# Sliding-window attention with a GeGLU branch: P times V by 64-key halves in two PSUM banks, row maxima in quarters of the TensorE array

## Chip, cores and metric

One core of a Trainium2 chip runs the whole kernel. The metric is the device time of one execution in microseconds (us), lower is better. The kernel before has a median of 1067.9 us over three runs (1067.76 to 1069.48).

Engines are named as the profile names them: PE is TensorE (PEld its weight loads), DVE VectorE, ACT ScalarE, POOL GpSimd, SP the engine that issues most DMAs. PE multiplies a moving operand by stationary weights, adds into PSUM banks, and can be split into row tiles (by the contracted dimension) and column tiles (by the output's partitions).

## What is computed

```python
def _A_ref(x, wqkv, wo):
    B, S, D = x.shape                       # 1, 2048, 640
    H = 32; Dh = D // H; W = 256            # 32 heads of 20, window of 256 keys
    qkv = (x @ wqkv).reshape(B, S, 3, H, Dh).transpose(2, 0, 3, 1, 4)
    q, k, v = qkv[0], qkv[1], qkv[2]
    scores = einsum("bhqd,bhkd->bhqk", q, k) * (Dh ** -0.5)
    mask = (0 <= idx[:, None] - idx[None, :]) & (idx[:, None] - idx[None, :] < W)
    p = softmax(where(mask, scores, -1e9), axis=-1)
    o = einsum("bhqk,bhkd->bhqd", p, v)
    return o.transpose(0, 2, 1, 3).reshape(B, S, D) @ wo

def _B_ref(x, w_gate, w_up, w_down):        # Df = 1728
    return (gelu(x @ w_gate) * (x @ w_up)) @ w_down

xn = layernorm(x)
return x + _A_ref(xn, ...) + _B_ref(xn, ...)
```

A query sees itself and the 255 keys before it, so only a band of the scores is computed.

## The kernel before

**Stages.** The first 60 us or so normalise and transpose x and start the projections. Then the attention stage (some 100 to 645 us in the profile) runs attention and the projections together. After it come the rest of the gate and up products and the output products. The change lies in the attention stage and in one mask that is built at the start.

**Units and slots.** Attention is cut into 32 units: 8 groups of 4 heads, times 4 chunks of 512 queries. `attention()` writes the order of PE, ACT, DVE and POOL out by hand: what the Python emits first stands first in each engine's queue. A unit has 14 slots (`NS`). In every slot come first the deferred actions that fall due (`tick`, filled by `defer(n, ...)`, n slots later), then the maxima, P times V and exp work of that slot, then about three steps of filler (`pull_fill(RATE / NS)`): matmuls of the projections and of the gate and up products, which are long, full-array f32r matmuls (L105).

**Maxima.** `max_pair(u, i)` (L458) computes the scores of two heads for 128 queries, only to find each query's maximum. The two heads lie in two row halves of the array (60 rows each, `tile_position=(64 * r, 0)`) and write two PSUM banks of `psm`, which has four. The band of 128 queries is 384 keys wide; where it reaches into the previous chunk the keys come from that chunk's tile in a matmul of their own. DVE adds the mask and reduces in one custom instruction for each head (L477). `pull_max(2, T)` emits two such calls at slots 0, 0, 4 and 8: the second of slot 0 behind P times V. So two calls take all four banks. The stream of maxima runs some units ahead.

**Exp.** `exp_piece(u, s)` (L518) computes the scores of one head again, transposed (keys on partitions), into a bank of `psx`, which has two, and ACT writes exp into a P tile (f32, 128 keys x 4 heads x 512 columns). A unit has three P tiles X, Z and Y of several key blocks each (`pieces`), so 12 pieces, two in every even slot from 0 to 10. One slot after a tile's last piece `clear` sets what lies outside the band to zero, on POOL (L545, L548). In slot 0 one step of filler stands between the two pieces.

**P times V.** `av_unit(u - 1)` (L551) runs in slot 0 between the two pulls of maxima. For each key block (128 keys on the partitions), for each of the 4 heads, one f32 matmul adds v-transposed times P into the head's 32 partitions of one `psx` bank `o` (column tiles 0, 32, 64, 96; the 21st row of v is ones and gives the sum). A chunk above 0 has six key blocks, with 384, 128, 256, 256, 384 and 128 queries; chunk 0 has four, with 384, 256, 384 and 128. ACT copies `o` to `ob`, and three slots later SP stores it with five DMAs.

Of the kernel before, what the change touches and what calls it, by code (L numbers as in the profile page):

```python
# [19 lines left out]
C = 512  # L20
# [7 lines left out]
NEG = -3.0e38  # L28
SR = 3 * DH
# [36 lines left out]
def block_kernel(ctx, tc, x, wqk, wv, wgu, wdo, wdl, out):  # L66
    nc = tc.nc
# [41 lines left out]
    def dense(*a):  # L109
        for _ in dense_steps(*a):  # L110
# [8 lines left out]
    qkp = pa.enter_context(tc.tile_pool(name="qkp", bufs=2))  # L119
    pr = ExitStack()  # L120
    vp = pr.enter_context(tc.tile_pool(name="vp", bufs=5, side="right"))
    st1 = pr.enter_context(tc.tile_pool(name="st1", bufs=1, side="right"))
    identb = st1.tile([128, 256], BF, name="identb")[:, 0:128]
    nc.gpsimd.tensor_copy(identb, ident)
    mask = st1.tile([128, 384], F32, name="mask")
    nc.gpsimd.memset(mask, 0.0)
    nc.gpsimd.affine_select(out=mask, in_=mask, pattern=[[1, 384]], compare_op=OP.is_ge,
                            fill=NEG, base=-1, channel_multiplier=-1)
    nc.gpsimd.affine_select(out=mask, in_=mask, pattern=[[-1, 384]], compare_op=OP.is_ge,
                            fill=NEG, base=256, channel_multiplier=1)  # L130
# [327 lines left out]
    def max_pair(u, i):  # L458
        g, c = divmod(u, NC)
        jj, b = divmod(i, 4)  # L460
        q, k = qs[u % NQ], ks[u % NK]
        if i == 0:
            maxes[u] = ap.tile([128, 4, 4], F32, name="mx", tag="mx")
        pss = [psm.tile([128, 384], F32, name="ps_m", tag="mx") for _ in range(2)]
        old = max(0, 256 - 128 * b) if c else 0
        n0 = max(0, 128 * b - 256)
        n = old + 128 * b + 128 - n0
        parts = [(0, old, ks[(u - 1) % NK], C - old, C)] if old else []
        parts.append((old, n, k, n0, 128 * b + 128))
        for lo, hi, kt, k0, k1 in sorted(parts, key=lambda p: p[1] - p[0]):  # L470
            for r, ps in enumerate(pss):
                rows, j = slice(64 * r, 64 * r + SR), 2 * r + jj
                nc.tensor.matmul(ps[:, lo:hi], q[rows, j, 128 * b:128 * b + 128], kt[rows, j, k0:k1],  # L473
                                 start=True, stop=True, tile_position=(64 * r, 0))
        junk = ap.tile([128, 384], BF, name="junk", tag="junk", bufs=1)
        for r, ps in enumerate(pss):
            nc.vector.tensor_tensor_reduce(out=junk[:, 0:n], in0=ps[:, 0:n], in1=mask[:, 384 - n:384], scale=1.0,  # L477
                                           scalar=NEG, op0=OP.add, op1=OP.max,
                                           accum_out=maxes[u][:, 2 * r + jj, b:b + 1])
# [70 lines left out]

    def av_unit(u):  # L551
        g, c = divmod(u, NC)
        o, v = psx.tile([128, C], F32, name="ps_o", tag="ex"), vtiles[g]
        todo = [(pts[u, bi], *p) for bi, bank in enumerate(pieces(c)) for p in bank]
        for i, (pt, kb, col, q0, n) in enumerate(todo):
            assert (id(v), kb) in done, (u, kb)
            for j in range(4):
                w0_ = kb * 84 + 21 * j
                nc.tensor.matmul(o[32 * j:32 * j + 32, q0:q0 + n], v[:, w0_:w0_ + 32], pt[:, j, col:col + n],  # L559
                                 start=i == 0, stop=i == len(todo) - 1, skip_group_check=True,  # L560
                                 tile_position=(0, 32 * j))
        ob = ap.tile([128, C], F32, name="ob", tag="ob", bufs=1)
        nc.scalar.activation(ob, o, AF.Copy)  # L563

        def store():
            for j in range(4):
                nc.sync.dma_start(od[c].rearrange("(d h) t -> h d t", h=H)[4 * g + j], ob[32 * j:32 * j + DH, :])
            nc.sync.dma_start(sd[c][4 * g:4 * g + 4, :], ob[DH::32, :])

        defer(3, store)  # L570

    def load_gu(f):
        raws = []
# [181 lines left out]
    def attention():  # L755
        now[0] = -1
        load_stack(0)
        load_stack(1)
        load_stack(2)
        for i, (p, k, half) in enumerate((p, k, half) for p in range(NC // 2) for k in range(2) for half in range(2)):  # L760
            for j, fn in enumerate(x_sums(p, k, half)):
                at(XS0 + XSN * i + 2 * j, fn)
        for i in range(12):
            now[0] = i - 13
            for fn, a in tick():
                fn(*a)
            if i % 2 == 0:
                pull_max(2, now[0])
            flush()
            pull_fill(2 * RAMP)  # L770
        pull_fill(GAP)
        for u in range(NU + 1):
            for i in range(NS):
                T = now[0] = NS * u + i
                for fn, a in tick():
                    fn(*a)
                if i in (0, 4, 8) or T == 2:
                    pull_max(2, T)
                if i == 0 and u:
                    av_unit(u - 1)  # L780
                    flush()
                    pull_max(2, T)
                if i % 2 == 0 and i < 12 and u < NU:
                    exp_piece(u, i)
                    if i == 0 and u:
                        pull_fill(1)
                        debt[0] -= 1
                    exp_piece(u, i + 1)
                flush()
                if u + 3 < NU and i in (KSLOT, 12):  # L790
# [661 lines left out]
```

## Time and profile before

| | |
|---|---|
| median of three runs | 1067.9 us |
| span of the profiled execution | 1070.0 us |
| instructions in the profile | 21147 |
| mean granted TensorE clock | 0.995 |
| P times V (L559): instructions, PE time | 1408, 84.3 us |
| maxima (L473): instructions, PE time | 704, 67.0 us |
| reductions on DVE (L477) | 512, 272.6 us |
| eviction of P times V on ACT (L563) | 32, 19.1 us |

The profile is one execution. A group's busy time counts overlapping instructions once, so the mean duration of one times the number is more than the busy time where several run at once. Matmuls are pipelined: the duration of one includes its way through the array, and what it costs in a row of others is read from differences of shapes or from the chain. The chain of waits follows the work that ended last back to what released it; its pieces are times that the end depended on.

### The profile page before, as it was taken

Reading aid. Unit: us, or ns where it says so; the run is one execution under the profiler, and the core shown is the slowest. Engines: PE = TensorE matmul, PEld = TensorE weight load, DVE = VectorE, ACT = ScalarE, POOL = GpSimd, SP = SyncE. Lnnn points to the kernel's source line nnn. Section 1 sums busy time; section 2 is a strip of 40 time slices with the busy share of each in tenths; the row PEclk is TensorE's granted clock in tenths of the full one; section 3 lists DMA queues with packets and bytes.
Section 4 is the critical chain, followed back from the end, with each engine's and each line's share of the span. In section 5 each row is a group of like instructions: output and inputs, shape, how many; then the busy total and the mean of one; then the engine's idle time right before and its main releaser. Section 6 shows DMA issues by size and latency. Waiting matters only on the chain.

```text
span 1070.0 us, 21147 instructions
## 1 busy us (share of the span) xinstructions
PE 1055.2 (99%) x7253; PEld 830.4 (78%) x7253; DVE 746.0 (70%) x1985; ACT 518.8 (48%) x1088; POOL 337.8 (32%) x514
## 2 busy tenths in 40 slices
PE   8999999999999999999999999999999999999998
PEld 8877666666677766666666668888888999999998
DVE  7845667665565566776767716787776879888887
ACT  4434565566556565565556565332234544433332
POOL 5021564767554383736346340211100000000000
PEclk9999999999999999999999999999999999999999
DMA  5642344446452244424334116576677873443443
GB/s 196 189 131 85 114 135 126 145 131 187 131 153 86 86 120 139 150 85 134 96 116 130 55 60 198 172 245 207 244 247 240 274 261 120 129 131 109 132 132 104
DMA packets 105172, 158.46 MB, mean 148 GB/s; under 512 B 15420, under 2 KB 60092, under 8 KB 105064
## 3 DMA queue, kind: packets, MB, share of 16 engines
q1 hardware_dynamic: 102680, 150.95, 44.5%
q10 hardware_dynamic: 2384, 6.16, 1.8%
q8 instruction: 57, 0.93, 0.4%
q14 instruction: 51, 0.42, 0.1%
HBM read 101.78 MB, written 54.92 MB: 146 GB/s over the span
## 4 chain that ended last, share of the span: by engine, by line
PE 86%; DVE 7%; DMA 2%; ACT 2%; issue 2%; POOL 1%; SPq 0%; ACTq 0%; DVEq 0%; POOLq 0%
PE ps_d L105 27%; PE ps L1168 16%; PE ps_g L901 15%; PE ps_e L532 8%; PE ps_o L559 6%; PE ps_v L105 6%; PE ps_m L473 5%; DVE junk L477 2%; PE ps_g L105 1%; DMA hr<-hd 1%; DVE ss L1006 1%; PE ps_t L180 1%; DVE wt L1006 1%; DVE at L1006 1%; ACT wb L987 1%
## 5 line engine op out<-in xcount | busy, mean ns | idle before, releaser
L477 DVE CUSTOM_DVE_ANT_0 junk<-ps_m,mask 128x384 bf16<-128x384 f32 (+2 forms) x512 | 272.6, 532 | 150.5 <-PE ps_m L473 92.7
L534 ACT ACTIVATE P<-ps_e 128x512 f32<-128x512 f32 (+2 forms) x384 | 198.5, 569 | 93.6 <-PE ps_e L532 79.9
L1168 PE MATMUL ps<-wb,at 128*128 128x320 f32 x999 | 156.7, 309 | 1.1 <-DVE xr L1191 0.7
L1168 PEld LDWEIGHTS ps<-wb,at 128*128 128x128 f32 x999 | 148.9, 188 | 2.1 <-issue 0.9
L545 POOL TENSOR_SCALAR_AFFINE_SELECT P<-P 128x512 f32<-128x512 f32 x128 | 86.1, 672 | 168.0 <-ACT P L534 165.7
L105 PE MATMUL ps_d<-xh,wql 128*128 128x512 f32 x430 | 130.5, 415 | 0.0
L105 PE MATMUL ps_d<-xh,wqh 128*128 128x512 f32 x430 | 129.2, 413 | 0.0
L105 PE MATMUL ps_d<-xl,wqh 128*128 128x512 f32 x430 | 129.2, 412 | 0.0
L532 PE MATMUL ps_e<-qs,ks 124*128 124x128 bf16 (+2 forms) x704 | 117.7, 279 | 0.2 <-ACT ob L563 0.2
L532 PEld LDWEIGHTS <-ks 124*128 124x128 bf16 x704 | 49.6, 98 | 60.5 <-issue 51.1
L105 PEld LDWEIGHTS ps_d<-xl,wqh 128*128 128x128 f32 x430 | 80.1, 191 | 14.8 <-issue 0.8
L105 PEld LDWEIGHTS ps_d<-xh,wql 128*128 128x128 f32 x430 | 80.0, 191 | 13.8
L105 PEld LDWEIGHTS ps_d<-xh,wqh 128*128 128x128 f32 x430 | 79.1, 189 | 15.0 <-ACT xh L188 1.4
L1168 PE MATMUL ps<-wt,at 128*128 128x320 f32 x552 | 89.2, 310 | 0.8 <-DVE xr L1191 0.8
L559 PE MATMUL ps_o<-P,v 128*32 128x384 f32 (+2 forms) x1408 | 84.3, 386 | 0.0
L1168 PEld LDWEIGHTS ps<-wt,at 128*128 128x128 f32 x552 | 82.9, 188 | 1.3 <-DVE xr L1191 1.0
L548 POOL TENSOR_SCALAR_AFFINE_SELECT P<-P 128x512 f32<-128x512 f32 x112 | 72.9, 661 | 28.7 <-ACT P L534 28.7
L1122 ACT ACTIVATE at<-ss 128x512 fp32r<-128x512 f32 x59 | 37.3, 632 | 88.3 <-DVE ss L1006 88.3
L244 POOL TENSOR_TENSOR pt<-r,pt 128x512 bf16<-128x512 f32 x40 | 46.6, 1164 | 90.7 <-ACT pt L243 76.9
L559 PEld LDWEIGHTS ps_o<-P,v 128*32 128x32 f32 x1408 | 41.4, 110 | 39.7 <-issue 25.1
L473 PE MATMUL ps_m<-ks,qs 60*128 60x128 bf16 (+1 forms) x704 | 67.0, 275 | 4.8 <-DVE mx L477 3.1
L563 ACT ACTIVATE ob<-ps_o 128x512 f32<-128x512 f32 x32 | 19.1, 597 | 93.2 <-PE ps_o L559 80.1
(189 smaller groups left out, 1682.4 us busy)
## 6 DMA issues: line engine op xcount, KB each, us to landing
hr<-hd SPq DMA_DIRECT2D x104, 128.0 KB
hd<-he SPq DMA_DIRECT2D x50, 256.0 KB
wr<-wgu SPq DMA_DIRECT2D x27, 320.0 KB
qs<-qd SPq DMA_DIRECT2D x64, 120.0 KB
ks<-kd SPq DMA_DIRECT2D x64, 120.0 KB
xi<-x SPq DMA_DIRECT2D x16, 320.0 KB
qs<-qd SPq DMA_DIRECT2D x64, 80.0 KB
ks<-kd SPq DMA_DIRECT2D x64, 80.0 KB
```

The source lines that it names most:

```text
L105: nc.tensor.matmul(ps, a(k), b(k), start=n == 0, stop=n == 3 * nk - 1)
L244: nc.gpsimd.tensor_tensor(out=pt[:, l, :], in0=r, in1=pt[:, 1, :], op=OP.subtract)
L473: nc.tensor.matmul(ps[:, lo:hi], q[rows, j, 128 * b:128 * b + 128], kt[rows, j, k0:k1], start=True, stop=True, tile_position=(64 * r, 0))
L477: nc.vector.tensor_tensor_reduce(out=junk[:, 0:n], in0=ps[:, 0:n], in1=mask[:, 384 - n:384], scale=1.0, scalar=NEG, op0=OP.add, op1=OP.max ...
L532: nc.tensor.matmul(ps[:, col:col + n], k[0:QROWS, j, kc:kc + 128], q[0:QROWS, j, q0:q0 + n], start=True, stop=True)
L534: nc.scalar.activation(pt[:, j, lo:hi], ps[:, lo:hi], AF.Exp, scale=SCALE)
L545: nc.gpsimd.affine_select(out=a, in_=a, pattern=[[0, 4], [1, 128]], compare_op=OP.is_ge, fill=0.0, base=0, channel_multiplier=-1)
L548: nc.gpsimd.affine_select(out=a, in_=a, pattern=[[0, 4], [-1, 128]], compare_op=OP.is_ge, fill=0.0, base=-1, channel_multiplier=1)
L559: nc.tensor.matmul(o[32 * j:32 * j + 32, q0:q0 + n], v[:, w0_:w0_ + 32], pt[:, j, col:col + n], start=i == 0, stop=i == len(todo) - 1, ski ...
L901: nc.tensor.matmul(ps, i, j, start=first and n == 0, stop=n == len(work) - 1, skip_group_check=True)
L1122: nc.scalar.activation(hi[:, 3:7], s, AF.Copy)
L1168: nc.tensor.matmul(ps[bank][:, 0:HD], *work[bank][j], start=bank not in begun, stop=final[p, bank] == n and j == len(work[bank]) - 1, skip ...
```

## The change

P times V takes the 128 keys of a block as two halves of 64, in two row tiles of the array, each half adding into a bank of its own (`os`, both banks of `psx`). A half reads only the queries that its 64 keys reach, at most 320. The halves are emitted in pairs of equal width (`steps_`). ACT copies both banks, the second into the first plane of the unit's third P tile; POOL adds the two three slots later, and the store moves from three slots later to five.

The maxima use four quarters of the array: two heads times two halves of 64 queries, with 320 keys each. Mask and reductions are 320 wide; the mask's lower 64 partitions are shifted against the upper ones and are built in a second tile. In the first two blocks of chunk 0, the columns without keys of the half are filled with a key repeated or with masked keys.

The exp pieces move from the even slots 0 to 10 to the odd slots 1 to 11.

```diff
-    mask = st1.tile([128, 384], F32, name="mask")
-    nc.gpsimd.memset(mask, 0.0)
-    nc.gpsimd.affine_select(out=mask, in_=mask, pattern=[[1, 384]], ..., base=-1, channel_multiplier=-1)
-    nc.gpsimd.affine_select(out=mask, in_=mask, pattern=[[-1, 384]], ..., base=256, channel_multiplier=1)
+    mask = st1.tile([128, 320], F32, name="mask")
+    low = qkp.tile([128, C], F32, name="r", tag="r", bufs=1)[:, 0:320]
+    for m, off in ((mask, 0), (low, 64)):
+        nc.gpsimd.memset(m, 0.0)
+        nc.gpsimd.affine_select(out=m, in_=m, pattern=[[1, 320]], ..., base=off - 1, channel_multiplier=-1)
+        nc.gpsimd.affine_select(out=m, in_=m, pattern=[[-1, 320]], ..., base=256 - off, channel_multiplier=1)
+    nc.gpsimd.tensor_copy(mask[64:128], low[64:128])
...
-        pss = [psm.tile([128, 384], F32, name="ps_m", tag="mx") for _ in range(2)]
-        old = max(0, 256 - 128 * b) if c else 0
-        n0 = max(0, 128 * b - 256)
-        n = old + 128 * b + 128 - n0
-        parts = [(0, old, ks[(u - 1) % NK], C - old, C)] if old else []
-        parts.append((old, n, k, n0, 128 * b + 128))
-        for lo, hi, kt, k0, k1 in sorted(parts, key=lambda p: p[1] - p[0]):
-            for r, ps in enumerate(pss):
-                rows, j = slice(64 * r, 64 * r + SR), 2 * r + jj
-                nc.tensor.matmul(ps[:, lo:hi], q[rows, j, 128 * b:128 * b + 128], kt[rows, j, k0:k1],
-                                 start=True, stop=True, tile_position=(64 * r, 0))
+        pss = [psm.tile([128, 320], F32, name="ps_m", tag="mx") for _ in range(2)]
+        n = 320 if c else min(320, 128 * b + 128)
+
+        def quarters(cut):
+            for h in range(2):
+                part = cut(128 * b + 64 * h - 256, 128 * b + 64 * h + 64)
+                for r, ps in enumerate(pss):
+                    if part is not None:
+                        kt, col, k0, k1 = part
+                        rows, j = slice(64 * r, 64 * r + SR), 2 * r + jj
+                        q0 = 128 * b + 64 * h
+                        ks_ = kt[rows, j, 0:1].to_broadcast([SR, 64]) if k0 == k1 else kt[rows, j, k0:k1]
+                        w = max(64, k1 - k0) if k0 == k1 else k1 - k0
+                        nc.tensor.matmul(ps[64 * h:64 * h + 64, col:col + w], q[rows, j, q0:q0 + 64], ks_,
+                                         start=True, stop=True, tile_position=(64 * r, 64 * h))
+
+        if c:
+            quarters(lambda lo, hi: (ks[(u - 1) % NK], 0, C + lo, C) if lo < 0 else None)
+        elif b < 2:
+            quarters(lambda lo, hi: (k, 320 - n, 0, 64 * b) if 320 - hi > 320 - n else None)
+        quarters(lambda lo, hi: (k, max(0, -lo), max(0, lo), hi))
...
-            nc.vector.tensor_tensor_reduce(out=junk[:, 0:n], in0=ps[:, 0:n], in1=mask[:, 384 - n:384], scale=1.0,
+            nc.vector.tensor_tensor_reduce(out=junk[:, 0:n], in0=ps[:, 320 - n:320], in1=mask[:, 320 - n:320], scale=1.0,
...
     def av_unit(u):
-        o, v = psx.tile([128, C], F32, name="ps_o", tag="ex"), vtiles[g]
-        todo = [(pts[u, bi], *p) for bi, bank in enumerate(pieces(c)) for p in bank]
-        for i, (pt, kb, col, q0, n) in enumerate(todo):
+        v = vtiles[g]
+        os = [psx.tile([128, C], F32, name="ps_o", tag="ex") for _ in range(2)]
+        place = {kb - 4 * c: (pts[u, bi], col, q0) for bi, bank in enumerate(pieces(c)) for kb, col, q0, n in bank}
+
+        def half(d, r):
+            i = 2 * d + r
+            return d, r, max(0, 64 * i), min(C, 64 * i + 320)
+
+        steps_ = [((0, 0), (0, 1)), ((2, 0), (-1, 1)), ((-1, 0), (2, 1)), ((1, 0), (1, 1)),
+                  ((3, 0), (-2, 1)), ((-2, 0), (3, 1))]
+        todo = [half(*x) for pair in steps_ for x in pair if x[0] in place]
+        begun_, left = set(), [sum(t[1] == r for t in todo) for r in range(2)]
+        for d, r, qa, qb in todo:
+            pt, col, q0 = place[d]
+            kb = 4 * c + d
+            left[r] -= 1
+            rows = slice(64 * r, 64 * r + 64)
             for j in range(4):
                 w0_ = kb * 84 + 21 * j
-                nc.tensor.matmul(o[32 * j:32 * j + 32, q0:q0 + n], v[:, w0_:w0_ + 32], pt[:, j, col:col + n],
-                                 start=i == 0, stop=i == len(todo) - 1, skip_group_check=True,
-                                 tile_position=(0, 32 * j))
-        nc.scalar.activation(ob, o, AF.Copy)
+                nc.tensor.matmul(os[r][32 * j:32 * j + 32, qa:qb], v[rows, w0_:w0_ + 32],
+                                 pt[rows, j, col + qa - q0:col + qb - q0], start=r not in begun_,
+                                 stop=not left[r], skip_group_check=True, tile_position=(64 * r, 32 * j))
+            begun_.add(r)
+        ob, oc = ap.tile([128, C], F32, name="ob", tag="ob", bufs=1), pts[u, 2][:, 0]
+        lo = 0 if c else 64
+        nc.scalar.activation(ob, os[0], AF.Copy)
+        nc.scalar.activation(oc[:, lo:], os[1][:, lo:], AF.Copy)
+
+        def join():
+            nc.gpsimd.tensor_tensor(out=ob[:, lo:], in0=ob[:, lo:], in1=oc[:, lo:], op=OP.add)
...
-        defer(3, store)
+        defer(3, join)
+        defer(5, store)
...
-                if i % 2 == 0 and i < 12 and u < NU:
-                    exp_piece(u, i)
-                    if i == 0 and u:
+                if i % 2 and i < 12 and u < NU:
+                    exp_piece(u, i - 1)
+                    if i == 1 and u:
                         pull_fill(1)
                         debt[0] -= 1
-                    exp_piece(u, i + 1)
+                    exp_piece(u, i)
```

More of the change, by code (lines that the diff above doesn't have):

```diff
@@ L124, in block_kernel @@
     nc.gpsimd.tensor_copy(identb, ident)
-    mask = st1.tile([128, 384], F32, name="mask")
-    nc.gpsimd.memset(mask, 0.0)
[L127 to L130, printed above, removed]
+    mask = st1.tile([128, 320], F32, name="mask")
+    low = qkp.tile([128, C], F32, name="r", tag="r", bufs=1)[:, 0:320]
+    for m, off in ((mask, 0), (low, 64)):
+        nc.gpsimd.memset(m, 0.0)
+        nc.gpsimd.affine_select(out=m, in_=m, pattern=[[1, 320]], compare_op=OP.is_ge,
+                                fill=NEG, base=off - 1, channel_multiplier=-1)
+        nc.gpsimd.affine_select(out=m, in_=m, pattern=[[-1, 320]], compare_op=OP.is_ge,
+                                fill=NEG, base=256 - off, channel_multiplier=1)
+    nc.gpsimd.tensor_copy(mask[64:128], low[64:128])
     pp = ExitStack()
@@ L475, in max_pair @@
-        junk = ap.tile([128, 384], BF, name="junk", tag="junk", bufs=1)
+        pss = [psm.tile([128, 320], F32, name="ps_m", tag="mx") for _ in range(2)]
[12 more added lines that the diff above has]
+                                         start=True, stop=True, tile_position=(64 * r, 64 * h))
@@ L476, in max_pair @@
+        if c:
[3 more added lines that the diff above has]
+        quarters(lambda lo, hi: (k, max(0, -lo), max(0, lo), hi))
+        junk = ap.tile([128, 320], BF, name="junk", tag="junk", bufs=1)
         for r, ps in enumerate(pss):
-            nc.vector.tensor_tensor_reduce(out=junk[:, 0:n], in0=ps[:, 0:n], in1=mask[:, 384 - n:384], scale=1.0,
+            nc.vector.tensor_tensor_reduce(out=junk[:, 0:n], in0=ps[:, 320 - n:320], in1=mask[:, 320 - n:320], scale=1.0,
@@ L552, in av_unit @@
         g, c = divmod(u, NC)
-        o, v = psx.tile([128, C], F32, name="ps_o", tag="ex"), vtiles[g]
-        todo = [(pts[u, bi], *p) for bi, bank in enumerate(pieces(c)) for p in bank]
-        for i, (pt, kb, col, q0, n) in enumerate(todo):
+        v = vtiles[g]
[11 more added lines that the diff above has]
+            kb = 4 * c + d
             assert (id(v), kb) in done, (u, kb)
+            left[r] -= 1
+            rows = slice(64 * r, 64 * r + 64)
             for j in range(4):
                 w0_ = kb * 84 + 21 * j
-                nc.tensor.matmul(o[32 * j:32 * j + 32, q0:q0 + n], v[:, w0_:w0_ + 32], pt[:, j, col:col + n],
-                                 start=i == 0, stop=i == len(todo) - 1, skip_group_check=True,
-                                 tile_position=(0, 32 * j))
-        ob = ap.tile([128, C], F32, name="ob", tag="ob", bufs=1)
-        nc.scalar.activation(ob, o, AF.Copy)
+                nc.tensor.matmul(os[r][32 * j:32 * j + 32, qa:qb], v[rows, w0_:w0_ + 32],
[8 more added lines that the diff above has]
+            nc.gpsimd.tensor_tensor(out=ob[:, lo:], in0=ob[:, lo:], in1=oc[:, lo:], op=OP.add)
         def store():
```

## The prediction, made before the changed kernel ran

> **What bounds the kernel now.** I read the busy times first, then the shares of the chain that ended last, then the busy times over the attention stage alone (100 to 645 us; the change touches nothing after it).
>
> ```profile
> PE 1055.2 (99%) x7253; PEld 830.4 (78%) x7253; DVE 746.0 (70%) x1985; ACT 518.8 (48%) x1088; POOL 337.8 (32%) x514
> ...
> PE 86%; DVE 7%; DMA 2%; ACT 2%; issue 2%; POOL 1%; SPq 0%; ACTq 0%; DVEq 0%; POOLq 0%
> ...
> 100.00:645.00 545.00, 541.37 (x4247) 362.74 (x4247) 341.93 (x1131) 315.07 (x676) 291.44 (x459) 1.00 0.39 118
> ```
>
> The columns of the last row are length, PE, weight loads, DVE, ACT, POOL, granted clock. PE is the bound in this stage, at full clock, with 3.6 us idle of 545; DVE, ACT and POOL have 200 us and more to spare each. So what leaves PE's queue leaves the time. The chain of waits through one unit (start, length, what) prices the two edited steps:
>
> ```profile
> 335.04 0.44 PE ps_m L473 x8
> 335.48 2.73 PE ps_o L559 x48
> 338.21 0.43 PE ps_m L473 x4
> 338.64 0.32 PE ps_e L532 x2
> 338.96 0.29 PE ps_v L105 x2
> 339.25 0.24 PE ps_e L532 x2
> ...
> 342.45 0.27 PE ps_m L473 x4
> ```
>
> P times V (L559) of a chunk above 0 takes 2.73 us for 48 instructions; two calls of the maxima (L473) 0.44 or 0.43 where they span 384 keys, 0.27 where the stream is in chunk 0's first two blocks. After a chunk 0 the chain runs elsewhere; PE and DVE in order of time:
>
> ```profile
> 385.93 2.15 PE L559 MATMUL ps_o<-P,v 128*32 128x384 f32 x32
> 388.00 0.93 PE L473 MATMUL ps_m<-ks,qs 60*128 60x384 bf16 x4
> ```
> ```profile
> 385.88 0.55 DVE junk L477
> ...
> 388.00 0.56 DVE junk L477
> ...
> 388.62 0.32 PE ps_m L473
> ```
>
> Here P times V starts a new engine step after 2.07 us, but the maxima behind it take 0.93 instead of 0.43: their last bank is released by the first of four reductions on DVE, 0.71 us apart (385.88 to 388.00 in three steps), and the fourth's end lets PE go on at 388.62. These 8 units are bound by DVE at this place.
>
> **P times V.** Durations by shape, first of PE, then of the reductions on DVE:
>
> ```profile
> L559 PE MATMUL ps_o<-P,v 128*32 128x384 f32 x512 | 53.8, 492 | 0.0
> L559 PE MATMUL ps_o<-P,v 128*32 128x256 f32 x448 | 30.0, 379 | 0.0
> L559 PE MATMUL ps_o<-P,v 128*32 128x128 f32 x448 | 22.5, 273 | 0.0
> ```
> ```profile
> 302.12 0.53 PE L559 MATMUL ps_o<-P,v 128*32 128x384 f32 x4
> ```
>
> 128 more columns cost 379 - 273 = 106 ns, 0.83 ns a column; each of the 704 calls is two instructions (1408), so a call costs 1.66 ns a column. The second row shows four instructions of some 0.5 us inside 0.53 us: the four heads of a piece, in four column groups, run together, each waiting only for its own group. The columns of a chunk above 0 are 384+128+256+256+384+128 = 1536, times 1.66 = 2.55 us, and 0.18 us of 2.73 is the change of array shape and the start. Chunk 0: 1152 columns, 1.91 us, of 2.07.
>
> After the change a call covers 64 keys and the two row halves of the array hold different key halves. If they run together, a chunk above 0 costs per head 320+256+192+320+128+64 = 1280 columns (the six pairs are of equal width), 2.12 us, and chunk 0 320+256+320+128 = 1024, 1.70 us. The rest I raise from 0.18 to 0.24, since each group of instructions is now eight and not four: 2.36 us, **0.37 less in 24 units, 8.9 us**. In the 8 units behind a chunk 0 PE would gain 0.15, but DVE decides there:
>
> ```profile
> L477 DVE CUSTOM_DVE_ANT_0 junk<-ps_m,mask 128x384 bf16<-128x384 f32 x425 | 236.9, 558 | 125.3 <-PE ps_m L473 77.5 <-DVE mx L477 0.5 <-PE ps_e L532 0.5
> ...
> L477 DVE CUSTOM_DVE_ANT_0 junk<-ps_m,mask 128x256 bf16<-128x256 f32 x28 | 11.9, 425 | 4.0
> ```
>
> (558 - 425) / 128 = 1.04 ns a column, so 320 instead of 384 saves 67 ns, four reductions 0.27 us: **8 x 0.27 = 2.1 us**. In the other units the same gate falls from 2.69 us after P times V begins (388.62 - 385.93) to 2.42, below the 2.5 at which PE now wants the last bank, so it stays hidden.
>
> Two things are not in the trace. The overlap of the row halves in f32: the nearest row is the maxima's, two row halves in bf16, whose four 384-column instructions took 0.43 us where one after another they would need four times 384 x 0.41 ns (the rows below), 0.63, and the change of shape on top; they overlap. And the feeding of twice as many instructions: 96 with 96 weight loads in 2.36 us is 24.6 ns a pair. Bounds: the four starts above lie within 0.02 us, 7 ns a pair; over the whole step 2.73/48 = 57 ns a pair were enough. I take the first, since the second is set by streaming.
>
> The TensorE page of the Trainium skill ("TensorE: Matmul & The Clock Gate", section "Wait — 56ns, not 53.3ns?") gives a floor of about 25 ns from matmul to matmul. By it 96 would take 2.4 us and the sum below would lose some 5 us of its gain; the 7 ns starts above disagree for different column groups.
>
> **Maxima.**
>
> ```profile
> L473 PE MATMUL ps_m<-ks,qs 60*128 60x384 bf16 x256 | 36.7, 327 | 3.3 <-DVE mx L477 2.6
> ...
> L473 PE MATMUL ps_m<-ks,qs 60*128 60x256 bf16 x224 | 25.8, 269 | 1.0 <-DVE xl L189 1.0
> ...
> L473 PE MATMUL ps_m<-ks,qs 60*128 60x128 bf16 x224 | 22.9, 222 | 0.5 <-DVE mx L477 0.5
> ```
>
> (327 - 222) / 256 = 0.41 ns a column. Two calls fall from 768 to 640 columns per array part: 0.05 us less of 0.44. There are 128 such doubles, 16 of them (chunk 0, blocks 0 and 1) unchanged in width: 112 x 0.053 = 5.9 us at most. Where keys of the previous chunk are needed the instructions double to 16 and some are 64 wide; for those 48 I bound the gain by 0 and 0.053 and take half: **4.6 us**, 3.4 at least.
>
> **What is added.**
>
> ```profile
> L563 ACT ACTIVATE ob<-ps_o 128x512 f32<-128x512 f32 x32 | 19.1, 597 | 93.2 <-PE ps_o L559 80.1 <-DMA qs<-qd 9.6 <-issue 3.3
> ```
> ```profile
> L244 POOL TENSOR_TENSOR pt<-r,pt 128x512 bf16<-128x512 f32 x30 | 34.9, 1164 | 26.8 <-ACT pt L243 21.8 <-DMA sd<-ob 4.7 <-DMA ks<-kd 0.4
> ```
>
> A second eviction on ACT, 32 x 0.597 = 19 us, and a joining add on POOL, 32 x about 1.16 = 37 us: both beside PE, on engines with 230 and 254 us free in the stage. The add reads oc, the first plane of the third P tile, which exp writes again at slot 9; the add is queued at slot 3. The store moves from slot 3 to 5, with its five DMAs on SP; ob is written again only at slot 14. Nothing waits on it sooner.
>
> P times V now takes both banks of psx, so the first exp waits for the first eviction and the second for the other. The move of exp from even to odd slots covers that. PE's next step and the eviction, each in order of time:
>
> ```profile
> 304.85 0.50 PE L473 MATMUL ps_m<-ks,qs 60*128 60x384 bf16 x4
> ```
> ```profile
> 304.98 0.60 ACT L563 ACTIVATE ob<-ps_o 128x512 f32<-128x512 f32 x1 [2.69 <-DMA qs<-qd]
> ```
>
> The eviction starts 0.13 us after PE has gone on; the first will end 0.73, the second 1.33 after that. PE meanwhile does 0.43 of maxima and three steps of filler, 0.228 each (12 in 2.74, rows below), 1.1 us; the second exp comes 0.61 later (338.64 to 339.25), at 1.7. Some 0.3 us of cover is left. Without it each unit would lose up to 0.6 us (an eviction). I put 0.6 us in all for ACT arriving late elsewhere.
>
> The move also brings the last exp one slot nearer to the P times V that reads it:
>
> ```profile
> 365.81 0.45 PE ps_e L532 x4
> 366.27 2.74 PE ps_d L105 x12
> 369.01 0.44 PE ps_m L473 x8
> 369.45 0.76 PE ps_o L559 x5
> ```
> ```profile
> 368.48 0.63 POOL L545 TENSOR_SCALAR_AFFINE_SELECT P<-P 128x512 f32<-128x512 f32 x1
> ```
> ```profile
> 386.37 0.64 POOL L545 TENSOR_SCALAR_AFFINE_SELECT P<-P 128x512 f32<-128x512 f32 x1
> ```
>
> Four slots of filler become three, 0.68 us. POOL's last mask of the third P tile ended at 369.11, 0.34 before P times V (369.45); in a loaded unit at 387.01, 1.08 after its start (385.93). That tile is first read as the fourth pair, 768 columns or 1.28 us in. So the usual unit keeps 0.9 us, the loaded one stalls 0.5. I count three such units with smaller ones: 1.2 us.
>
> At the start POOL builds two masks of 320 instead of one of 384:
>
> ```profile
> 1.65 0.51 POOL L127 TENSOR_SCALAR_AFFINE_SELECT mask<-mask 128x384 f32<-128x384 f32 x1
> ...
> 11.92 3.07 POOL L287 TENSOR_TENSOR wvl<-wvall,wvh 128x320 fp32r<-128x320 f32 x3 [6.27 <-ACT wvh L286]
> ```
>
> About 1.5 us more, in a gap of 6.27: nothing.
>
> **The sum.** 8.9 + 2.1 + 4.6 - 0.6 - 1.2 = 13.8 us. The profiled execution spans 1070.0, so 1056.2; the unprofiled runs have a median of 1067.9, 2.1 lower, so **1054 us**.
>
> **Rivals.**
>
> *Halves a step apart.* If a row half can begin only when the half queued before it has started its second instruction, the halves run one instruction apart and each pair costs its own width plus the wider of its own and the last: (320+320)+(320+256)+(256+192)+(320+320)+(320+128)+(128+64)+64 = 3008 half-columns, times 0.83 = 2.50 us against 2.55. P times V gains 32 x 0.05 = 1.6, the maxima 4.6, the stalls cost 1.8: 4.4 less, **1063.5 us**. For it: the window over which PE looks ahead must be twice as long. Against: the four starts within 0.02 us already pass over the second instruction of each head.
>
> The same page ("Part 3: Packing small matmuls — row/col tiling") says that matmuls start in strict program order. By that rule this rival would hold at the least; those four starts disagree with it, since the call for the second head stands behind both instructions of the first.
>
> *Feeding becomes the bound, slower.* If PE can't take up a weight load and a matmul every 24.6 ns, P times V is 96 pairs times that price. It is as long as before at 2.73/96 = 28 ns; the maxima and costs shift the balance to about 30. At the trace's upper bound of 57 ns it is 5.5 us in 24 units and 64 x 57 = 3.65 in 8: 24 x 2.74 + 8 x 1.58 = 78 us, less 2.8 of the rest, **1143 us**; at 35 ns, 24 x 0.63 + 8 x 0.17 = 16.5 less 2.8, 1081.6 us. For it: no stretch shows so dense a stream for long. Against: the 7 ns.
>
> *The halves don't overlap at all.* Then 2560 columns take 4.25 us, in chunk 0 1920 take 3.19: 24 x 1.7 + 8 x 1.28 - 2.8 = 48 us, 1116 us. Against: the maxima's row halves.
>
> *It doesn't come to the end of PE's queue.* The exps, late by the evictions, give back 32 x 0.4: about 1067. Against: ACT's 230 us.
>
> **Chances.** Forecast 0.62; halves a step apart or in part 0.15; given back 0.06; feeding 0.10; no overlap 0.07. The likeliest one's own range is 1049 (5.9 for the maxima, no stalls, DVE's gate open) to 1059. To leave out no more than 0.2 it must take in the second and third: 1048 to 1069. A measurement of this kernel can tell 0.2%, 2.1 us, from no change. Faster: 0.62 + 0.14 = 0.76; same 0.05; slower 0.19.
>
> **What would show it.** Right: P times V at 2.3 to 2.4 us in the chain with 96 instructions, eight starting within 0.06 us; the double maxima at 0.38; the reductions at 491 ns; the exp pieces of odd slots with no idle from ACT's evictions. Wrong: P times V at 2.5 or more, with the halves' starts a whole instruction apart (second rival) or evenly spaced by 28 ns or more (feeding); PE waiting on POOL's masks in most units and not in three; more slices of lower granted clock.

## The result, and the profile after

The changed kernel takes 1068.4 us (median of 20 runs, 1064.3 to 1072.0), the kernel before, run beside it, 1069.3 us. The ratio is 0.9991, with a 95% interval from 0.9978 to 1.0004: no change that this measurement can tell. The forecast was 1054 us.

Busy times of the changed kernel, then the reductions by line (busy time, mean ns, idle time before):

```profile
PE 1052.9 (99%) x9429; PEld 832.7 (78%) x9429; DVE 722.9 (68%) x1985; ACT 531.1 (50%) x1120; POOL 375.6 (35%) x550
...
L490 DVE CUSTOM_DVE_ANT_0 junk<-ps_m,mask 128x320 bf16<-128x320 f32 (+2 forms) x512 | 243.0, 475 | 171.7 <-PE ps_m L480 114.1
```

PE is as full as before, with 2176 instructions more, and DVE has 23 us less to do. The chain of waits through one unit (start, length, what) shows both edits doing what they were costed for, and one thing besides:

```profile
332.38 0.40 PE ps_m L480 x8
332.78 2.38 PE ps_o L586 x93
335.16 0.69 PE ps_m L480 x8
335.85 0.93 PE ps_v L105 x5
336.78 0.23 PE ps_e L545 x2
...
343.17 0.73 PE ps_v L105 x5
343.91 0.40 PE ps_m L480 x8
344.30 0.92 PE ps_v L105 x5
345.22 0.45 PE ps_e L545 x4
345.68 1.33 PE ps_v L105 x9
347.01 0.46 PE ps_e L545 x4
347.46 2.05 PE ps_v L105 x14
349.51 0.30 PE ps_m L480 x8
```

P times V (L586) is down from 2.73 to 2.38 us, the double maxima (L480) from 0.44 to 0.40. (The 0.69 behind P times V is a wait on DVE in this unit; more of it below.) But compare the rows of five filler steps (L105): behind exp they take 0.73, behind the maxima 0.92 or 0.93. In the kernel before, exp stood behind the maxima and filler behind exp:

```profile
346.42 0.43 PE ps_m L473 x4
346.85 0.54 PE ps_e L532 x4
347.40 1.33 PE ps_v L105 x9
```

There the exp behind the maxima takes 0.54 where four matmuls of exp behind filler take 0.45. So whoever follows the maxima pays: exp 0.09, filler 0.19.

To see what this sums to I took PE's matmuls from the start of the second P times V to that of the last (30 units), cut them into runs of one result tile, and counted each run from its first start to the start of the next run. The filler in these units is the same work in every kernel (1110 matmuls of 512 columns and 240 of 320), so its differences are lost time. All in us; "places" are the runs of filler that stand right behind maxima or behind the one-instruction step `ps_n` (L507), which stands ahead of an exp as well:

| kernel | places | P times V | maxima | exp | ps_n | filler | 30 units |
|---|---|---|---|---|---|---|---|
| before | 0 | 77.3 | 53.3 | 51.3 | 1.9 | 326.6 | 510.5 |
| after | 114 | 70.3 | 48.1 | 52.3 | 1.1 | 337.6 | 509.4 |

P times V, maxima and `ps_n` gave 13.0 us, exp and filler took 12.0 back. The row of the kernel before needs a correction: its trace has a granted clock of 0.5 from 269.2 to 272.6 us, while filler and exp run, which costs 1.7 us (some 1.4 of filler and 0.3 of exp). The kernel after has no such stretch in these units. Without it the row before would have 325.2 of filler, 51.0 of exp and 508.8 in all, and exp and filler take 13.7 back: in these units the change gains nothing. (The profile before spans 4.8 us more than the one after; 1.1 of it is in the table as read, the rest lies ahead of the second P times V and behind the last, where the change does little. The medians differ by 0.9.)

### The profile page after: what moved, and what is told of

Its sections match the earlier page's. It is cut to its first block, busy times and chain, and to the rows that moved or that the text cites. A ratio compares the mean times of both kernels' runs of the same rounds, so it can differ in the third digit from the quotient of the medians.

```text
span 1065.2 us, 25614 instructions
## 1 busy us (share of the span) xinstructions
PE 1052.9 (99%) x9429; PEld 832.7 (78%) x9429; DVE 722.9 (68%) x1985; ACT 531.1 (50%) x1120; POOL 375.6 (35%) x550
## 4 chain that ended last, share of the span: by engine, by line
PE 84%; DVE 5%; POOL 4%; DMA 3%; issue 2%; ACT 2%; SPq 0%; ACTq 0%; DVEq 0%; POOLq 0%
PE ps_d L105 25%; PE ps L1202 19%; PE ps_g L935 16%; PE ps_e L545 7%; PE ps_v L105 6%; PE ps_o L586 5%; PE ps_m L480 4%; PE ps_g L105 1%; POOL pt L247 1%; DVE junk L490 1%; DMA xi<-x 1%; POOL P L561 1%; POOL P L558 1%; DVE ss L1040 1%; DMA hr<-od 1%
## 5 line engine op out<-in xcount | busy, mean ns | idle before, releaser
L490 DVE CUSTOM_DVE_ANT_0 junk<-ps_m,mask 128x320 bf16<-128x320 f32 (+2 forms) x512 | 243.0, 475 | 171.7 <-PE ps_m L480 114.1
L105 PE MATMUL ps_d<-xh,wql 128*128 128x512 f32 x430 | 136.7, 421 | 0.0
L105 PE MATMUL ps_d<-xh,wqh 128*128 128x512 f32 x430 | 135.1, 419 | 0.0
L105 PE MATMUL ps_d<-xl,wqh 128*128 128x512 f32 x430 | 134.8, 418 | 0.0
L558 POOL TENSOR_SCALAR_AFFINE_SELECT P<-P 128x512 f32<-128x512 f32 x128 | 82.2, 642 | 101.9 <-ACT P L547 99.5
L105 PEld LDWEIGHTS ps_d<-xl,wqh 128*128 128x128 f32 x430 | 77.4, 189 | 15.4 <-issue 3.4
L105 PEld LDWEIGHTS ps_d<-xh,wql 128*128 128x128 f32 x430 | 77.0, 189 | 15.7 <-issue 3.6
L105 PEld LDWEIGHTS ps_d<-xh,wqh 128*128 128x128 f32 x430 | 76.7, 189 | 15.5 <-issue 3.1
L561 POOL TENSOR_SCALAR_AFFINE_SELECT P<-P 128x512 f32<-128x512 f32 x112 | 70.8, 642 | 35.4 <-ACT P L547 35.4
L586 PE MATMUL ps_o<-P,v 64*32 64x320 f32 (+4 forms) x2816 | 75.9, 348 | 0.9 <-POOL P L561 0.6
L586 PEld LDWEIGHTS ps_o<-P,v 64*32 64x32 f32 x2816 | 48.5, 106 | 26.6 <-POOL P L558 3.4
L480 PE MATMUL ps_m<-ks,qs 60*64 60x320 bf16 (+3 forms) x1472 | 63.3, 260 | 2.6 <-DVE xl L192 1.1
L480 PEld LDWEIGHTS <-qs 60*64 60x64 bf16 x1472 | 28.3, 105 | 42.1 <-issue 36.7
```

Source lines behind the costliest of these rows:

```text
L105: nc.tensor.matmul(ps, a(k), b(k), start=n == 0, stop=n == 3 * nk - 1)
L480: nc.tensor.matmul(ps[64 * h:64 * h + 64, col:col + w], q[rows, j, q0:q0 + 64], ks_, start=True, stop=True, tile_position=(64 * r, 64 * h))
L490: nc.vector.tensor_tensor_reduce(out=junk[:, 0:n], in0=ps[:, 320 - n:320], in1=mask[:, 320 - n:320], scale=1.0, scalar=NEG, op0=OP.add, op ...
L558: nc.gpsimd.affine_select(out=a, in_=a, pattern=[[0, 4], [1, 128]], compare_op=OP.is_ge, fill=0.0, base=0, channel_multiplier=-1)
L561: nc.gpsimd.affine_select(out=a, in_=a, pattern=[[0, 4], [-1, 128]], compare_op=OP.is_ge, fill=0.0, base=-1, channel_multiplier=1)
L586: nc.tensor.matmul(os[r][32 * j:32 * j + 32, qa:qb], v[rows, w0_:w0_ + 32], pt[rows, j, col + qa - q0:col + qb - q0], start=r not in begun ...
```

## The experiments

Ten more kernels ran, each beside the kernel before on the same chip.

**Undoing the order alone.** If the filler behind the maxima takes the gain, moving exp back behind the maxima gives it back with all of the rest kept; moving it away in the old kernel must cost as much there. `e1_even` is the kernel after with exp behind the maxima wherever the two evictions allow it (the first pair stays in slot 1, since P times V holds its banks in slot 0):

```diff
-                if i % 2 and i < 12 and u < NU:
-                    exp_piece(u, i - 1)
+                if i in (1, 3, 4, 6, 8, 10) and u < NU:
+                    s = i - i % 2
+                    exp_piece(u, s)
...
-                    exp_piece(u, i)
+                    exp_piece(u, s + 1)
```

> The changed kernel with its exp pieces back on even slots, except the first pair, which stays at slot 1, and the second at 3: slots 1, 3, 4, 6, 8, 10. At slots 4 and 8 exp stands directly behind the maxima again and at slot 6 behind the transposed maxima. Theory (filler behind the maxima): the change's own gain of some 12 us is given back because an f32r filler matmul behind the maxima shows its weight load, 0.1 us each, in 88 places of the attention stage, and because the later exp makes P times V wait for POOL some 2.5 us in all. This kernel keeps the wait in 30 of the 88 places, so it should be 8 to 11 us faster than the changed kernel: ratio to the kernel before 0.989 to 0.992. Rival (the slots of exp cost nothing; the time went elsewhere, for example to the doubled instructions): the same as the changed kernel, 0.997 to 1.001. Rival (the evictions of two banks hold the exps, so that closer spacing hurts): slower than the changed kernel, above 1.002.

Measured 1060.2 us, ratio 0.9921 (0.9900 to 0.9941).

`e2_odd` is the kernel before with exp moved to the odd slots, as the change moved it, and nothing else:

```diff
-                if i % 2 == 0 and i < 12 and u < NU:
-                    exp_piece(u, i)
-                    if i == 0 and u:
+                if i % 2 and i < 12 and u < NU:
+                    exp_piece(u, i - 1)
+                    if i == 1 and u:
...
-                    exp_piece(u, i + 1)
+                    exp_piece(u, i)
```

> The kernel before with nothing changed but the slots of exp, odd instead of even. Theory (filler behind the maxima): 88 filler entries behind maxima and 30 behind the transposed maxima, about 0.1 us each, with some waits for POOL: 9 to 13 us slower, ratio 1.008 to 1.012. Rival (slots of exp cost nothing): 0.998 to 1.002.

Measured 1079.6 us, ratio 1.010 (1.008 to 1.012). Its chain of waits has the same 0.92 behind the old maxima:

```profile
331.71 0.43 PE ps_m L473 x4
332.14 0.92 PE ps_v L105 x5
333.07 0.45 PE ps_e L532 x4
```

`e3_gap` is the kernel before with exp left in its even slots and one step of filler put between the maxima and exp:

```diff
                 if i % 2 == 0 and i < 12 and u < NU:
+                    if i in (0, 4, 8) and u:
+                        pull_fill(1)
+                        debt[0] -= 1
                     exp_piece(u, i)
```

> The kernel before with exp on its even slots, but with one filler matmul, taken from the slot's own, between maxima and exp at slots 0, 4 and 8. Nothing is later by more than 0.25 us, so POOL and the banks are as before. Theory: 90 to 96 entries of filler behind the maxima, each 0.10 to 0.13 us: 9 to 12 us slower, ratio 1.008 to 1.012. Rival (what costs in the changed kernel is the lateness of exp, not its place behind filler): 0.998 to 1.002.

Measured 1080.0 us, ratio 1.0095 (1.0073 to 1.0117).

All three came out at the edge of the theory's bounds or within them: filler right behind the maxima is the cost, by itself and with either form of maxima. The move of exp cost 1.0% in the old kernel, and undoing 85 of its 114 places gave 0.7% back in the new one. That exp is later, or nearer to its reader, isn't the cost: in `e3_gap` it is in its old slots. (One thing more changes in `e3_gap`: the step of filler between the two exps of slot 0 falls away, so that these stand together.) The loads of weights in order of time show what is paid; first the kernel after, where filler follows maxima, then the kernel before, where exp does:

```profile
344.23 0.30 PEld L105 LDWEIGHTS ps_v<-wvh,xh 128*128 128x128 f32 x2 [0.25 <-issue]
344.49 0.19 PEld L105 LDWEIGHTS ps_v<-wvh,xl 128*128 128x128 f32 x1
```
```profile
346.78 0.33 PEld L532 LDWEIGHTS <-ks 124*128 124x128 bf16 x4 [0.32 <-issue]
347.07 0.35 PEld L105 LDWEIGHTS ps_v<-wvh,xh 128*128 128x128 f32 x2
```

A filler load takes 0.188 us, an exp load 0.098. The first load behind the maxima starts only when the change of shape is over (344.23, the same instant as its matmul). The loads within one unbroken stretch of filler are issued ahead, beside the running matmuls. Behind the maxima the second load starts 0.11 after the first, and the second filler matmul 0.250 us after the first instead of the usual 0.143 to 0.148: 0.107 lost. In the old order the second exp matmul starts 0.066 after the first, where 0.053 is its 128 columns: 0.013 lost (behind filler it is the same, 0.067); and the filler's first load (347.07) starts while exp still streams. So the change of shape costs some 0.09 in both orders, and the filler pays about 0.1 more. I read this as a long f32 load that nothing covers; no run separates the load's length from what else sets filler apart from exp (f32, 128 rows). Times 114 (85 places behind maxima and 29 behind `ps_n`, none of which the old order has) 0.107 is 12.2 us; the filler column has 337.6 - 325.2 = 12.4. The new order also changes from filler to exp 115 times more often, but that is free: the last filler matmul ahead of exp takes the usual 0.146 (344.919 to 345.065 in the kernel after).

The Trainium skill ("TensorEngine Tiling (Array Packing)", section "Key Properties") says that a change of tiling mode drains TensorE. The 0.09 us behind the maxima agree with a drain; the further 0.1 is this trace's own.

**The two parts alone.** `e4_max` has the new maxima and masks, with P times V and the exp slots of before:

```diff
-                nc.tensor.matmul(ps[:, lo:hi], q[rows, j, 128 * b:128 * b + 128], kt[rows, j, k0:k1],
-                                 start=True, stop=True, tile_position=(64 * r, 0))
+                        nc.tensor.matmul(ps[64 * h:64 * h + 64, col:col + w], q[rows, j, q0:q0 + 64], ks_,
+                                         start=True, stop=True, tile_position=(64 * r, 64 * h))
```

> The maxima of the changed kernel (quarters, 320 keys, mask of 320) alone, with P times V in one bank and exp on even slots as before. From the traces two calls take 0.40 instead of 0.44 us in the chain, and the reductions 67 ns less each: theory 4 to 6 us faster, ratio 0.994 to 0.997. Rival (the doubled instructions cost as much as the columns save): 0.999 to 1.001.

Measured 1060.6 us, ratio 0.9927 (0.9909 to 0.9946): more than expected, and as much as `e1_even`, which has the halves of P times V as well. `e5_pv` is the other part, P times V by halves with the exp slots of `e1_even` and the old maxima:

```diff
-                nc.tensor.matmul(o[32 * j:32 * j + 32, q0:q0 + n], v[:, w0_:w0_ + 32], pt[:, j, col:col + n],
+                nc.tensor.matmul(os[r][32 * j:32 * j + 32, qa:qb], v[rows, w0_:w0_ + 32],
+                                 pt[rows, j, col + qa - q0:col + qb - q0], start=r not in begun_,
```

> P times V of the changed kernel (halves, two banks, second eviction, add on POOL) alone, with the maxima of the kernel before and exp at slots 1, 3, 4, 6, 8, 10. Theory: the step itself is some 10 us shorter in all (0.35 us in 24 units, 0.22 in 8), but 30 filler matmuls now stand behind the maxima of slot 0 (0.18 us each in the changed kernel's trace, 5.3 us), and the second maxima of slot 0, which wait for the four reductions on DVE, wait longer by most of what P times V got shorter (3 to 5 us): ratio 0.997 to 1.002. Rival (the shorter step reaches the end, the wait for DVE is small): 0.993 to 0.996.

Measured 1068.9 us, ratio 0.9998 (0.9983 to 1.0012). The account, as above:

| kernel | places | P times V | maxima | exp | ps_n | filler | 30 units |
|---|---|---|---|---|---|---|---|
| e1_even | 29 | 68.0 | 51.5 | 51.8 | 1.9 | 329.6 | 502.8 |
| e2_odd | 114 | 78.0 | 50.5 | 51.8 | 1.1 | 337.7 | 519.1 |
| e3_gap | 85 | 77.3 | 52.9 | 55.1 | 1.9 | 330.3 | 517.5 |
| e4_max | 0 | 77.3 | 48.5 | 51.0 | 1.9 | 324.8 | 503.6 |
| e5_pv | 29 | 68.1 | 59.2 | 51.7 | 1.9 | 328.4 | 509.3 |

The trace of `e1_even` has a stretch at a granted clock of 0.5 too (265.5 to 268.9 us, 1.7 us, most of it filler); 501.1 would be left without it. With the clock of the kernel before put right, filler, exp and `ps_n` together take 378.1 us before, 387.3 in `e3_gap`, 390.6 in `e2_odd` and 391.0 after: 0.11 us for each place in all three, with the places behind `ps_n` (`e2_odd`, after) and without them (`e3_gap`). In `e3_gap` not quite half of it stands in the exp column only because two exps of slot 0 are now one run, whose streaming is no longer counted with the filler behind the first.

The halves save 9.2 us of P times V in `e5_pv`, and the maxima take 5.9 more. Those behind P times V wait for DVE, which releases their last bank:

```profile
336.00 2.38 PE ps_o L573 x93
338.38 0.56 PE ps_m L473 x4
338.94 0.92 PE ps_v L105 x5
```

0.56 instead of 0.43 here, 0.855 on average over the 30 units, against 0.666 before and 0.562 in `e4_max`. P times V was DVE's time to catch up: what it gets shorter, PE waits behind it. In 19 ordinary units the maxima behind P times V went from 0.438 to 0.537 on average, in 6 behind a chunk 0 from 0.89 to 1.12; in units 7 to 10 they took 7.7 us together against 5.4. Then filler stands behind these maxima, since exp can't (29 places).

**Giving DVE the time back.** In `e6_spread` (from `e1_even`) and `e7_spread_one` (from `e4_max`) the pulls of maxima stand in slots 0 (behind P times V), 3, 6 and 10, and no two pulls follow each other with only P times V between:

```diff
-                if i in (0, 4, 8) or T == 2:
-                    pull_max(2, T)
                 if i == 0 and u:
                     av_unit(u - 1)
                     flush()
-                    pull_max(2, T)
+                if i in (0, 3, 6, 10):
+                    pull_max(2, T)
```

Also `MXD`, by which the stream of maxima runs ahead, goes from 6 to 5, and `e7_spread_one` has exp in slots 0, 3, 4, 6, 8 and 10.

> The changed kernel with exp at slots 1, 3, 4, 6, 8, 10 and the four pulls of maxima spread: behind P times V at slot 0, and directly before exp at slots 3, 6 and 10, none before P times V (transposed maxima 5 slots behind instead of 6). Theory (in slot 0 the second pull waits for the reductions of the first; a pull there takes 0.645 us to the next step against 0.40 elsewhere): 30 x 0.245 = 7 us faster than with the pulls at 0, 0, 4, 8: ratio to the kernel before 0.984 to 0.988. Rival (that wait is not on the path): 0.991 to 0.994.

Measured 1059.0 us, ratio 0.9898 (0.9877 to 0.9920): between theory and rival.

> The maxima of the changed kernel with P times V in one bank as before, the pulls spread to slots 0, 3, 6, 10 and exp at slots 0, 3, 4, 6, 8, 10. Beside the kernel with the pulls spread and P times V by halves it shows what the halves are worth once the wait for DVE is gone. Theory: the wait in slot 0 is 0.15 us for 30 pulls, 5 us: ratio 0.987 to 0.990; the halves are then worth 10 us less 5 for the filler behind the maxima, so the other kernel is 3 to 6 us faster than this one. Rival (P times V by halves has a cost of its own that no wait shows): the two the same, or this one faster.

Measured 1065.1 us, ratio 0.9954 (0.9941 to 0.9968): a miss, slower than `e4_max`. The wait on DVE was gone in both (0.38 behind P times V); what had come in its place shows in the chain of `e6_spread`:

```profile
332.55 0.40 PE ps_m L480 x8
332.94 0.54 PE ps_e L545 x4
333.48 0.73 PE ps_v L105 x5
334.22 0.60 PE ps_e L545 x4
```

The exp of slot 4 stands 1.28 us behind that of slot 3 and takes 0.60 where 0.45 is usual: it finds its two banks still full, since ACT needs 0.60 us for each exp of a full bank. Over 30 units this group takes 0.483 on average, and 0.316 in `e4_max`. That it is ACT stands in the shares of this chain, where the exp on ACT has 5%:

```profile
by line: PE ps_v L105 57.2%; PE ps_e L545 19.7%; PE ps_o L586 10.8%; PE ps_m L480 8.1%; ACT P L547 5.0%; PE ps_n L507 0.3%; issue 0.3%
```

`e8_five` and `e9_five_one` move the third pair of exps by a slot:

```diff
-                if i in (1, 3, 4, 6, 8, 10) and u < NU:
+                if i in (1, 3, 5, 6, 8, 10) and u < NU:
```

`e10_pv_spread` is `e8_five` with the old maxima.

> The spread kernel with the third pair of exps one slot later (slots 1, 3, 5, 6, 8, 10). In the spread kernel the fourth group of exps, one slot behind the third, takes 0.483 us on PE on average over 30 units, the same group 0.316 to 0.330 where 1.6 us lie between the two: it waits until ACT has emptied its banks. Theory: with 1.6 us between them the wait goes, 30 x 0.16 = 5 us: ratio 0.983 to 0.987. Rival: ACT is late as a whole and the wait comes back at the next group of exps: 0.988 to 0.991, as the spread kernel.

Measured 1053.3 us, ratio 0.9859 (0.9840 to 0.9878): as the theory had it.

> The same shift in the spread kernel without the halves of P times V (exps in slots 0, 3, 5, 6, 8, 10). That kernel came out at 0.9954, and its fourth group of exps takes 0.484 us against 0.316 in the kernel with the new maxima alone. Theory: 30 x 0.17 = 5 us come back: 0.989 to 0.992. Rival, the loss comes from the extra change of array shape ahead of P times V alone: 0.994 to 0.997.

Measured 1061.1 us, ratio 0.9934 (0.9918 to 0.9950): between the two. The exp came back, and the order still brings nothing to this kernel beside `e4_max`.

> The halves of P times V with the old maxima (128 queries by 384 keys), in the order of the first kernel of this call. Theory: the gate on DVE is open in this order, so that the halves bring their 9 us even with the wide reductions; the old maxima cost 0.03 us in each of 113 places, 3.4 us: ratio 0.986 to 0.991. Rival: the wide reductions (0.53 us, four of them between two places two slots apart) keep DVE late, and PE waits behind the maxima as in the kernel with the halves alone: 0.993 to 1.0.

Measured 1058.2 us, ratio 0.9916 (0.9896 to 0.9935): between the two and nearer to the theory; its interval touches the rival's range, but the trace has no wait behind P times V (at most 0.44 us for the maxima there).

| kernel | places | P times V | maxima | exp | ps_n | filler | 30 units |
|---|---|---|---|---|---|---|---|
| e6_spread | 29 | 67.7 | 44.3 | 56.2 | 1.9 | 331.9 | 502.0 |
| e7_spread_one | 0 | 77.3 | 44.3 | 56.0 | 1.9 | 328.7 | 508.3 |
| e8_five | 29 | 67.7 | 44.4 | 51.6 | 1.9 | 331.4 | 497.0 |
| e9_five_one | 0 | 77.3 | 44.3 | 51.7 | 1.9 | 328.0 | 503.2 |
| e10_pv_spread | 29 | 68.5 | 47.8 | 51.6 | 1.9 | 331.8 | 501.7 |

`e9_five_one` beside `e4_max`: the maxima give 4.2 us (no wait on DVE), the filler takes 3.2, because P times V now has filler ahead of it and not maxima: in this trace the last filler matmul (512 columns) takes 0.085 us longer ahead of maxima or P times V than ahead of exp, and there are 29 more such places, 2.5 us. `e8_five` beside `e9_five_one` is what the halves bring once nothing else waits: 9.6 us of P times V less 3.4 of filler behind the maxima of slot 0, 6.2 us. `e8_five` beside `e10_pv_spread` is what the new maxima bring: 3.4 of 4.7 (of the rest, 0.7 is one stall of P times V in `e10_pv_spread`, in unit 16). In the chain of `e8_five` the unit is clean:

```profile
338.10 2.38 PE ps_o L586 x93
340.48 0.29 PE ps_m L480 x8
340.77 0.93 PE ps_v L105 x5
...
343.50 0.40 PE ps_m L480 x8
343.89 0.54 PE ps_e L545 x4
344.44 1.32 PE ps_v L105 x9
345.76 0.45 PE ps_e L545 x4
```

## Why the prediction was wrong

**The halves of P times V: right.** 2.376 us in the units above chunk 0 where nothing stalls, 2.36 predicted. Eight matmuls start at once, as forecast; PE in order of time, then the group of this shape (busy, mean ns):

```profile
332.72 0.50 PE L586 MATMUL ps_o<-P,v 64*32 64x320 f32 x8
```
```profile
L586 PE MATMUL ps_o<-P,v 64*32 64x320 f32 x1024 | 49.3, 436 | 0.9 <-POOL P L561 0.6
```

One takes 0.436 on average, all eight together 0.50; in the records they start between 332.716 and 332.763. So the halves don't run a step apart (2.50) and don't run one after the other. Feeding isn't the bound either: 2.376/96 is 24.8 ns a pair, which looks like the 25 ns floor of the Trainium skill ("TensorE: Matmul & The Clock Gate", section "Wait — 56ns, not 53.3ns?"), but those eight starts are 47/7 = 6.7 ns apart, and the 32 instructions more of a unit above chunk 0 against chunk 0 cost 2.376 - 1.86 = 0.52 us, nearer to the 0.42 of streaming their 256 columns than to 32 x 25 = 0.80. That page's strict order of starts ("Part 3: Packing small matmuls — row/col tiling") would have given the 2.50 at the least if, as the prediction takes it, the two instructions of a call stand together in the queue; the measured step doesn't agree with it. (The loss of 5 us that the prediction works out from the 25 ns comes out only with the change of shape on top of the 2.4 us; by 2.4 alone it is 24 x 0.04, 1 us.)

**Behind a chunk 0: right.** P times V and the maxima behind it together went from 2.08 + 0.86 to 1.86 + 0.86 us, 0.22 less; 0.27 was predicted. "It stays hidden" in the other units held in most (0.40 behind P times V), and failed where DVE came late: in units 3 and 13 (0.67 and 0.69) and 9 and 10 (1.03 and 0.53).

**Maxima: 4.6 predicted, less than half of it found in their width.** The double calls ahead of exp or filler went from 0.414 to 0.387 us on average, those ahead of P times V from 0.396 to 0.384: 58 x 0.027 + 30 x 0.012 = 1.9 us, and 0.2 in 19 ordinary units behind P times V. Calls in chunk 0's first blocks got longer, 0.27 to 0.30. The other 3.1 of the 5.2 in the account came in units 7 to 10 (5.4 to 2.4 us), from a wait that the prediction had not seen. The chain of the kernel before, in unit 9, whose P times V begins at 263.59:

```profile
263.16 0.69 POOL tx L690
263.85 1.14 POOL pt L244
264.99 0.02 issue
265.01 0.69 DVE r L258
265.70 0.46 DVE junk L477
...
267.74 0.56 DVE junk L477
...
268.36 0.32 PE ps_m L473
```

POOL is behind with its queue in these units, DVE waits for its add (L244), the four reductions come two microseconds late, and PE waits for the last. It stays in `e1_even` (5.3 us), is less in the kernel after (2.4, where P times V itself stalls on POOL in units 7, 8 and 10) and is gone in `e8_five` (1.5 us for four calls, no wait). Why POOL falls behind just there I did not test.

**POOL's masks: three units predicted, six found.** The idle time of P times V's weight loads, by what ended it:

```profile
  POOL P L561: 3.9, 8
  POOL P L558: 3.4, 9
```

In units 1, 6, 7, 8, 10 and 11 P times V took 2.65 to 2.83 us (unit 8 is a chunk 0, where 1.86 is usual); 2.5 us in all against the 1.2 forecast. In `e1_even`, with the last exp back in slot 10, the 7.3 us of these two rows fell to 0.7.

**The failed step: the move of exp.** The prediction says "The move of exp from even to odd slots covers that" (the wait for the evictions), and so it was: no group of exps waits there. It priced the move by what it hides and by POOL's deadline, and put the new order of work on PE itself at nothing, without a row for it. The order isn't neutral: the old order put exp, with short bf16 loads, behind every change of shape, the new one filler, with f32 loads. 114 places by some 0.11 us are the 12.4 us of filler (13.7 with exp) that ate the gain. The row of 0.32 instead of 0.24 for exp behind the maxima (338.64 and 339.25) was in the prediction's own fence; what stands behind a change of shape was never asked.

The rival that the exps give the gain back ended near the measured time, and it is this rival that stretched the stated range (1048 to 1069) to take in 1068.4. That was luck, since the mechanism is another: exp itself lost 1.3 us and not 32 x 0.4, and not by late evictions.

The sum with the measured terms, over the 30 units: 7.0 (P times V with its stalls) + 5.2 (maxima) + 0.8 (`ps_n`) - 1.3 (exp) - 12.4 (filler) = -0.7 us, where 13.8 were forecast (1.0 with the half-clock stretch of the trace before left in). That `e8_five` ends at 1053.3, beside the forecast of 1054, doesn't make the forecast right: of its 11.8 us in the account (508.8 - 497.0) the halves give 9.6, but the maxima 8.9, most of it waits on DVE that the prediction left in place or had not seen, and 6.2 are lost in filler and 0.6 in exp.

## What to carry to other kernels

When work is moved on a full PE, ask for each place where the array changes its shape what comes next: put the instruction with the short weight load there (here exp, 0.098 us), and let the long loads (filler, 0.188) stand behind matmuls of their own shape. A step that gets shorter may have been another engine's time to catch up; look at the wait behind it first, and respread that engine's work together with the change. Here the same two edits bring nothing in the order in which they were made, and 1.4% (1053.3 us) in another.

## What the hardware showed beyond that

- Eight f32 matmuls in parts of 64 by 32 run side by side in two banks, all eight in 0.50 us where one takes 0.436: 2.376 us for 96, where 48 in parts of 128 by 32 took 2.73.
- A change of array shape has no single price. In front of exp it is 0.09 us, in front of filler 0.19 (five steps: 0.92 against 0.73). The way into the parts costs as well: the last filler matmul takes 0.085 us longer ahead of maxima than ahead of exp (`e9_five_one`).
- The parts of the gain don't add. The new maxima alone gave 0.9927, the halves alone 0.9998, both in that order 0.9921; respread, the halves are worth 0.9859 against 0.9934.
